# Gated mix of Hedgehog attention and a Mish MLP: a reordered third chunk of projections, and row sums kept by adding DMAs

## The chip, the core and the metric

The kernel runs on one core of a Trainium2 chip. The metric is the device time of one execution in microseconds; the median of three runs of the kernel before is 460.61 us (460.45 to 461.32).

## What is computed

`x` has 2048 rows of 512; H is 32 heads of 16 columns, F is 1376.

```
qkv   = x @ wqkv
phi_q = [softmax(q w_phi), softmax(-q w_phi)]        per head, 32 features
phi_k = [softmax(k w_phi), softmax(-k w_phi)]
kv    = sum over rows of phi_k^T v ;  z = sum over rows of phi_k
a     = (phi_q kv) / (phi_q z + 1e-6) @ wo
b     = mish(x @ w1 + b1) @ w2
out   = g a + (1 - g) b ,   g = sigmoid(x . gate_w)
```

All is float32. Each float32 operand is split into a high and a low float32r part, and a product of two operands is three products on TensorE: high with high, high with low, low with high.

## The kernel before

`w_phi` is first multiplied into the keys' and queries' weights ("fuse"). Then the rows go by in eight chunks of 256 (stage A), each chunk in two tiles of 128 rows (`t` = 0, 1). For each tile the keys `k`, the values `v` and the queries `q` are projected; `mx`, `mn`, `d0`, `d1`, `E`, `S`, `rS` and `ml` make phi_k of the keys: largest and smallest of a head, two differences into the tile `E`, its exponential on ScalarE, the sums `Sm`, their reciprocals and the scaling `ml`. Queries go to DRAM (`pqd`). `kv` multiplies `E` with the values' copy `v` into one PSUM tile `kvp`, for two chunks at a time. After that come four blocks of 512 rows (stage B), in which TensorE does `up` (x w1), `down` (w2), `num` and `wo` back to back.

Every operation is recorded under a short name and a chunk. The texts FIRST, SECOND, STRASSEN, THIRD, NEXT, LAST and BLOCK0 to BLOCK name the operations in the order in which they are issued, and each engine and each DMA queue keeps that order. In a text `'` means the chunk before, `+` the first block, `#` the weights.

**The chunks with 66 products.** Chunks 2, 3 and 4 (FAST) get keys and queries of both tiles from seven products instead of eight (Strassen's scheme). A step `s1` to `s7` is one of them: six TensorE instructions, which the helper `term` issues. The products use sums of x (`sraw`, four POOL adds in `sa`), split into `sh` (ScalarE, steps sh0 and sh1) and `sl` (POOL, sl0 and sl1), and sums of the weights (t1 to t4, split by h0 to h3 into `th` or `sh`, and by l0 to l3 into `tl` or `sl`). t2 and l2 are VectorE's, h2 is ScalarE's. The steps between the products are

- `bc`: ScalarE copies PSUM tile k0, which holds s1, to q0; s2 goes on adding to k0, and s6, s5 and s3 to q0
- `m7`: ScalarE copies s7 (`m` in the profile)
- `ca`: VectorE adds q0 and `m` into the PSUM tile of k1, to which s4 adds
- `kk`: the kv products of chunks 0 and 1 (in chunk 2) or 2 and 3 (in chunk 4)
- `v0`, `v1`: the values' projection, twelve instructions each; `ve0` and `ve1` copy it from PSUM
- `xh`, `xl`: the split of the next chunk's x on ScalarE and VectorE

Buffers matter in two places. Tiles `E` have four buffers. Tiles of tag "io" have four too: three constants of the start take the first three, then each values' copy `v` takes the next, so that the copy of chunk 2's first tile takes the buffer of chunk 0's first.

**The sums z.** `zd0` and `zd1` are DRAM tiles of 128 x 1024 (512 KB). Steps `z0` and `z1` add each `E` to them with a DMA that adds (`accum_op`; POOL issues these). In chunk 6 `zld` reads zd0 into the SBUF tile `zacc` (queue of SP), `za` adds zd1 to it with an adding DMA, and POOL adds the four `E` of chunks 6 and 7 with tensor instructions. `zh` (ScalarE) and `zl` (VectorE) split `zacc` into `zs`; `@z` in BLOCK0 is the product with ones on TensorE, whose copies to SBUF are `zb`.

Of the kernel before, what the change touches and what calls it, by code (L numbers as in the profile page):

```python
# [12 lines left out]
ALU = mybir.AluOpType  # L13
# [10 lines left out]
NCH = S // SC  # L24
# [10 lines left out]
FAST = range(2, 5)  # L35
# [6 lines left out]
    S0 rS0 ml0 S1 rS1 ml1 q0 qe0 st0 q1 qe1 st1  # L42
"""
SECOND = """
    h0# h1# l0# h3# l1# l3# z0' z1' k0 xh mx0 mn0 d00 d10 xl sa ldx k1 E0 L0# L1# mx1 mn1 d01 d11 v0 E1 S0 rS0 ve0 ml0 t2# h2# sh0 sl0 z0
    v1 S1 rS1 ml1 ve1 q0 qe0 st0 q1 sh1 sl1 qe1 st1 l2#
"""
STRASSEN = """
    s1 bc s7 m7 kk s2 xh xl sa z1' mx0 mn0 s6 ca d00 d10 E0 ldx v0 ve0 sh0 sl0 more S0 rS0 s4 mx1 mn1 s5 qa st1 d01 d11 E1 ml0 z0
    v1 S1 rS1 s3 ve1 qe0 st0 ml1 sh1 sl1  # L50
"""
THIRD = """
    k0 z1' xh xl mx0 mn0 d00 d10 ldx k1 H6# E0 O6# L8# mx1 mn1 d01 d11 v0 H7# E1 O7# L9# S0 rS0 ml0 ve0 v1 H8# O8# L10# z0
    S1 rS1 ml1 ve1 q0 qe0 st0 q1 z1 qe1 st1 kv' kv
"""
NEXT = """
    lq0+ k0 xh xl mx0 mn0 d00 d10 ldx zld k1 H9# E0 O9# ldw0 L11# mx1 mn1 d01 d11 H10# E1 O10# ldw1 za S0 rS0 ml0 z0 v0 ve0 H11# O11#
    S1 rS1 ml1 z1 v1 ve1 q0 mx0+ mn0+ d00+ d10+ qe0 st0 q1 qe1 st1 E0+ lq1+
"""
LAST = """  # L60
    k0 mx0 mn0 d00 d10 k1 E0 XH0 kv' mx1 mn1 d01 d11 E1 v0 S0 rS0 ml0 z0 ve0 ldo XH1 mx1+ mn1+ d01+ d11+ E1+
    S1 rS1 ml1 z1 XL0 XL1 v1 ve1 lq2+ q0 WH0 qe0 st0 q1 WH1 zh qe1 st1 zl kv S0+ rS0+ km
"""


# [29 lines left out]
def tile_gated_mix(ctx: ExitStack, tc: tile.TileContext, xT, wv, wkT, wqT, bd, w1a, w1b, b1, w2a, w2b, wo, out):  # L95
# [6 lines left out]
    pin = tc.keep_in_program_order  # L102
    SYNC = mybir.DependencyInfo(mybir.DependencyClass.Sync, mybir.DependencyReason.DATA)
    V, G_, A_, Sy = nc.vector, nc.gpsimd, nc.scalar, nc.sync

    def mm(*a, **k):
        return pin(nc.tensor.matmul(*a, **k))  # L107
# [14 lines left out]
    def psum(name, tag, bufs={"a": 3, "dn": 4, "kv": 1}):  # L122
        nm[0] += 1
        return pp.tile([P, 512], F32, name=f"{name}_{nm[0]}", tag=tag, bufs=bufs[tag])

    def act(out_, in_, fn=AF.Copy, **k):
        return pin(A_.activation(out_, in_, fn, **k))  # L127
# [88 lines left out]
    Z = {}  # L216
# [117 lines left out]
    def fast_ops(c, key, P_):  # L334

        def x(k, t):
            return [xs[c][i][k][:, :, t * P : (t + 1) * P] for i in range(2)]

        def s(i):
            return [SX[j][:, i, :, :] for j in range(2)]  # L340

        def term(name, a, w, start, stop):
            n = 0
            for ai, wi in ((0, 0), (0, 1), (1, 0)):
                for k in range(2):
                    mm(P_[name], a()[ai][:, k, :], w[wi][:, k, :], start=(start and n == 0), stop=(stop and n == 5), skip_group_check=True)
                    n += 1

        def new(*k, tag="a"):
            P_[k if len(k) > 1 else k[0]] = psum("proj", tag)  # L350

        def s1_():
            new("k", 0)
            new("m7", tag="dn")
            term(("k", 0), lambda: x(0, 0), wk0, True, False)

        def bc():
            new("q", 0, tag="dn")
            act(P_["q", 0], P_["k", 0])

        def s7():
            term("m7", lambda: s(0), t3, True, True)

        def m7():
            P_["m7s"] = k2("m7", "pq")
            act(P_["m7s"], P_["m7"])

        def ca():
            new("k", 1)
            pin(V.tensor_add(P_["k", 1], P_["q", 0], P_["m7s"]))  # L370
# [12 lines left out]
    def a_ops(c):
        key = ("A", c)
        P_ = psA[c] = {}
        for t in range(2):
            d = {}
            Es[c, t] = d

            def k_(t=t):  # L390
                P_["k", t] = proj(xs[c], t, wkh, wkl, "a")

            def v_(t=t):
                P_["v", t] = proj(xs[c], t, wvh, wvl, "dn" if c or t else "kv")
# [24 lines left out]
            at(key, f"ve{t}", ve)
            if t and c in FAST:  # L420
                at(key, "qa", qa)
            else:
                at(key, f"qe{t}", qe)
            at(key, f"st{t}", st)
            feat_ops(key, t, lambda t=t: P_["k", t][:, :], d, t == 1 and c in FAST)
            at(key, f"ml{t}", lambda d=d: scale_by(d, V))
            def zs(t=t, d=d):
                if c >= NCH - 2:
                    pin(G_.tensor_add(Z["acc"], Z["acc"], d["E"]))
                elif c:  # L430
                    pin(G_.dma_start(zd[t][:, :], d["E"], accum_op=ALU.add))
                else:
                    pin(G_.dma_start(zd[t][:, :], d["E"]))
# [24 lines left out]
        if odd + 1 in FAST:
            at(("A", odd + 1), "kk", kv)
        else:  # L460
            at(key, "kv", kv)
        if c in FAST:
            fast_ops(c, key, P_)
        if c + 1 in FAST:
            fast_operands(c + 1, key)
        if c + 1 < NCH:
            def xh():
                new_x(c + 1)
                for j in range(2):
# [315 lines left out]
    acc = {}  # L785
# [63 lines left out]

    run(FIRST, ("A", 0))  # L850
    run(SECOND, ("A", 1), ("A", 0))
    for c in FAST:
        w = {2: "H0# O0# L2# H1# O1# L3#", 3: "H2# O2# L4# H3# O3# L5#", 4: "H4# O4# L6# H5# O5# L7#"}[c]
        run(STRASSEN.replace("more", w), ("A", c), ("A", c - 1))
    for c, text in ((NCH - 3, THIRD), (NCH - 2, NEXT), (NCH - 1, LAST)):
        run(text, ("A", c), ("A", c - 1), ("B", 0))
    for b in range(NB):
        run((BLOCK0, BLOCK1, BLOCK, BLOCK)[b], ("B", b), ("B", b - 1), ("B", b + 1))
# [61 lines left out]
```

## Time and profile before

| what | value |
|---|---|
| median of the runs | 460.61 us |
| profiled execution | 462.78 us |
| its span | 460.7 us |
| TensorE (PE) busy | 445.1 us, 97% |
| VectorE (DVE) busy | 322.2 us, 70% |
| ScalarE (ACT) busy | 205.9 us, 45% |
| GpSimd (POOL) busy | 162.9 us, 35% |
| DMA | 47.40 MB, mean 103 GB/s |

Times in the profile's rows are microseconds from the start of the span. Stage A ends near 158 us. "PE" is TensorE, "SPq" the DMA queue of SP. A bracket at the end of a row gives the engine's idle time before it and what ended that. An adding DMA shows on POOL only as the time of its issue (some 0.9 us); when its data have landed is a row of its own in the chain of waits.

### The profile page before, as it was taken

The page shows a single profiled execution, that of the slowest core. Times are in us where ns is not written, and L with a number is a line of the kernel's source. Part 1 is how long each engine was busy: PE and PEld are TensorE (multiplying, and loading weights), DVE is VectorE, ACT ScalarE, POOL GpSimd, SP SyncE. Part 2 cuts the span into 40 slices and gives each one's busy share as a digit, 9 for nine tenths or more (in the row PEclk, how much of TensorE's full clock was granted, in tenths as well). Part 3 has the DMA queues.
Part 4 walks back from the last instruction along what each step waited for, and adds up shares of the span by engine and source line. Part 5 has one row for each costly group of instructions (what it writes and reads, how often), then busy time and mean ns, then how long its engine had stood idle before and what let it go on. Part 6 is the DMA issues. An engine that isn't in the chain of part 4 may idle for free.

```text
span 460.7 us, 7012 instructions
## 1 busy us (share of the span) xinstructions
PE 445.1 (97%) x2754; PEld 362.1 (79%) x2754; DVE 322.2 (70%) x422; ACT 205.9 (45%) x286; POOL 162.9 (35%) x115
## 2 busy tenths in 40 slices
PE   7999599999999899999899999999999999999996
PEld 7888388888888678878687887887887888787885
DVE  2498878989596999979996985747967718621002
ACT  3753544735436373735338253353354552334220
POOL 2299758835625437130204203023212121321211
PEclk9999799999999999999999999999999999999999
DMA  7310766879595210222534042323041312030002
GB/s 284 152 46 0 280 134 172 181 194 285 150 311 138 79 47 1 69 70 59 149 89 161 1 110 73 94 73 108 11 127 48 108 30 91 1 75 19 0 0 91
DMA packets 27608, 47.40 MB, mean 103 GB/s; under 512 B 5940, under 2 KB 14132, under 8 KB 27576
## 3 DMA queue, kind: packets, MB, share of 16 engines
q1 hardware_dynamic: 25528, 39.88, 28.4%
q0 software_dynamic: 1904, 6.82, 7.3%
q8 instruction: 21, 0.34, 0.3%
q10 hardware_dynamic: 144, 0.26, 0.2%
q14 instruction: 11, 0.09, 0.1%
HBM read 23.87 MB, written 14.69 MB: 84 GB/s over the span
## 4 chain that ended last, share of the span: by engine, by line
PE 71%; DVE 8%; POOL 8%; DMA 7%; issue 3%; ACT 2%; POOLq 0%
PE up L107 25%; PE down L107 24%; PE wo L107 10%; PE proj L107 9%; DMA zacc<-zd 3%; DMA zd<-E 2%; PE fuse L107 2%; PE num L107 2%; DVE Sm L275 2%; DMA raw<-in_w2a_dram 1%; DVE E L286 1%; DMA bds<-in_bd_dram 1%; PE kvp L107 1%; POOL tl L307 1%; DVE xbl L535 1%
## 5 line engine op out<-in xcount | busy, mean ns | idle before, releaser
L630 POOL TENSOR_TENSOR l<-act,h 128x512 fp32r<-128x512 f32 x44 | 61.8, 1405 | 223.1 <-ACT h L127 188.3
L127 ACT ACTIVATE act<-up,b1s 128x512 f32<-128x512 f32 x44 | 30.3, 689 | 91.5 <-PE up L107 91.3
L127 ACT ACTIVATE E<-E 128x1024 f32<-128x1024 f32 x32 | 33.7, 1062 | 59.2 <-DVE E L271 41.2
L286 DVE TENSOR_TENSOR E<-E,Sm 128x1024 f32<-128x1024 f32 x32 | 43.6, 1362 | 1.0
L275 DVE TENSOR_REDUCE Sm<-E 128x64 f32<-128x1024 f32 x32 | 38.7, 1210 | 7.3 <-ACT E L127 7.3
L107 PE MATMUL wo<-woh,ohl 128*128 128x512 f32 x128 | 40.9, 390 | 1.2 <-DVE ohl L739 1.2
L107 PE MATMUL down<-w2ah,h 128*128 128x512 f32 x96 | 37.5, 390 | 0.0
L107 PE MATMUL down<-w2ah,l 128*128 128x512 f32 x96 | 37.4, 389 | 0.0
L107 PE MATMUL down<-w2al,h 128*128 128x512 f32 x96 | 37.3, 389 | 0.0
L765 DVE SCALAR_TENSOR_TENSOR io<-down,og_sb,io 128x512 f32<-128x512 f32 x16 | 11.3, 750 | 31.1 <-PE down L107 31.0
L107 PE MATMUL down<-w2bh,h 128*128 128x512 f32 x80 | 31.2, 390 | 0.0
L107 PE MATMUL down<-w2bl,h 128*128 128x512 f32 x80 | 31.1, 389 | 0.0
L107 PE MATMUL down<-w2bh,l 128*128 128x512 f32 x80 | 31.1, 389 | 0.0
L107 PEld LDWEIGHTS wo<-woh,ohl 128*128 128x128 f32 x128 | 24.0, 188 | 6.6 <-DVE ohl L739 1.6
L127 ACT ACT_TABLE_LOAD x19 | 24.4, 1283 | 10.1 <-PE up L107 9.8
L739 DVE TENSOR_TENSOR ohl<-num,ohl 128x512 fp32r<-128x512 f32 x16 | 10.2, 678 | 26.4 <-ACT ohl L127 26.4
L127 ACT ACTIVATE h<-act 128x512 fp32r<-128x512 f32 x44 | 27.8, 632 | 1.4
L107 PE MATMUL up<-xbl,w1ah 128*128 128x512 f32 x96 | 25.8, 390 | 1.7 <-DVE xbl L535 1.7
L107 PE MATMUL up<-xbh,w1ah 128*128 128x512 f32 x96 | 26.3, 396 | 0.2 <-ACT zb L127 0.2
L535 DVE TENSOR_TENSOR xbl<-xraw,xbh 128x1024 fp32r<-128x1024 f32 x8 | 12.2, 1562 | 19.8 <-ACT xbh L127 19.8
L107 PE MATMUL up<-xbh,w1al 128*128 128x512 f32 x96 | 25.7, 389 | 0.0
L107 PE MATMUL wo<-wol,ohl 128*128 128x512 f32 x64 | 24.9, 389 | 0.0
(155 smaller groups left out, 1018.6 us busy)
## 6 DMA issues: line engine op xcount, KB each, us to landing
xraw<-in_xT_dram SPq DMA_DIRECT2D x16, 512.0 KB, 5.2
eT<-tt SPq DMA_DIRECT2D x128, 64.0 KB, 2.0
zd<-E POOLq DMA_DIRECT2D x12, 512.0 KB, 7.2
pqd<-qs SPq DMA_DIRECT2D x16, 256.0 KB, 4.7
pq<-pqd SPq DMA_DIRECT2D x16, 256.0 KB, 2.9
out_dram<-io SPq DMA_DIRECT2D x16, 256.0 KB, 2.1
raw<-in_w1a_dram SPq DMA_DIRECT2D x3, 512.0 KB, 4.3
raw<-in_w2a_dram SPq DMA_DIRECT2D x3, 512.0 KB, 4.6
```

Source lines behind the costliest of these rows:

```text
L107: return pin(nc.tensor.matmul(*a, **k))
L127: return pin(A_.activation(out_, in_, fn, **k))
L275: pin(V.tensor_reduce(d["S"], hv(d["E"][:, :]), axis=AX.X, op=ALU.add))
L286: pin(eng.tensor_mul(hv(d["E"][:, :]), hv(d["E"][:, :]), d["S"][:, :, None].to_broadcast([P, 2 * H, DH])))
L307: at("W", f"l{i}", lambda i=i, r=r: pin((V if i == 2 else G_).tensor_sub(hl[1][i], r, f32(hl[0][i]))))
L535: pin(V.tensor_sub(xb[b][1][:, :, sl], kt(raw[h], SC), f32(xb[b][0][:, :, sl])))
L630: pin(G_.tensor_sub(U[i]["l"], U[i]["a"], f32(U[i]["h"])))
L739: pin(V.tensor_sub(ohl[h, gp][:, 512:], num[h, gp], f32(ohl[h, gp][:, :512])))
L765: pin(V.scalar_tensor_tensor(io[t], dn[t], og_sb[:, i : i + 1], io[t], op0=ALU.mult, op1=ALU.add))
```

## The change

1. In chunk 1 (SECOND) x's sums `sa` are added ahead of the DMAs z0 and z1 of chunk 0; sh0 and sl0 stand ahead of t2 and h2; t2 stands behind ml1, and h2 and l2 behind st0.
2. Chunk 2 gets a text of its own (THIRD; the old THIRD is now SIXTH). It begins with s1, bc, v0, ve0; `kk` comes after `ca`; both E0 and E1 come ahead of the weights' splits H0, O0, H1 and O1.
3. `term` issues high-high, low-high, high-low instead of high-high, high-low, low-high, in all three chunks.
4. z0 and z1 of chunk 6 add to zd0 and zd1 by DMA as the earlier ones; zld and za move to chunk 7, behind ml0; z0 and z1 of chunk 7 are adding DMAs from `E` straight into `zacc`. `zh` stands behind st1, and `zl` behind the first queries' S and rS.

```
 SECOND = """
-    h0# ... l3# z0' z1' k0 xh mx0 mn0 d00 d10 xl sa ldx k1 ... S0 rS0 ve0 ml0 t2# h2# sh0 sl0 z0
-    v1 S1 rS1 ml1 ve1 q0 qe0 st0 q1 sh1 sl1 qe1 st1 l2#
+    h0# ... l3# k0 xh mx0 mn0 d00 d10 xl sa z0' z1' ldx k1 ... S0 rS0 ve0 ml0 sh0 sl0 z0
+    v1 S1 rS1 ml1 t2# ve1 q0 qe0 st0 h2# l2# q1 sh1 sl1 qe1 st1
+THIRD = """
+    s1 bc v0 ve0 s7 m7 s2 xh xl sa z1' mx0 mn0 s6 ca kk d00 d10 E0 ldx sh0 sl0 s4 mx1 mn1 s5 qa st1 d01 d11 E1 H0# O0# L2# S0 rS0 ml0 z0
+    v1 H1# O1# L3# S1 rS1 s3 ve1 qe0 st0 ml1 sh1 sl1
 STRASSEN = """
     s1 bc s7 m7 kk s2 xh xl sa z1' mx0 mn0 s6 ca d00 d10 E0 ldx v0 ve0 sh0 sl0 more S0 rS0 s4 mx1 mn1 s5 qa st1 d01 d11 E1 ml0 z0
 NEXT = """
-    lq0+ k0 ... ldx zld k1 ... ldw1 za S0 rS0 ml0 z0 v0 ve0 H11# O11#
+    lq0+ k0 ... ldx k1 ... ldw1 S0 rS0 ml0 z0 v0 ve0 H11# O11#
 LAST = """
-    k0 ... S0 rS0 ml0 z0 ve0 ldo XH1 mx1+ mn1+ d01+ d11+ E1+
-    S1 rS1 ml1 z1 XL0 XL1 v1 ve1 lq2+ q0 WH0 qe0 st0 q1 WH1 zh qe1 st1 zl kv S0+ rS0+ km
+    k0 ... S0 rS0 ml0 ldo zld za z0 ve0 XH1 mx1+ mn1+ d01+ d11+ E1+
+    S1 rS1 ml1 z1 XL0 XL1 v1 ve1 lq2+ q0 WH0 qe0 st0 q1 WH1 qe1 st1 zh kv S0+ rS0+ zl km

-            for ai, wi in ((0, 0), (0, 1), (1, 0)):
+            for ai, wi in ((0, 0), (1, 0), (0, 1)):

-                if c >= NCH - 2:
-                    pin(G_.tensor_add(Z["acc"], Z["acc"], d["E"]))
+                if c == NCH - 1:
+                    pin(G_.dma_start(Z["acc"], d["E"], accum_op=ALU.add))
                 elif c:
                     pin(G_.dma_start(zd[t][:, :], d["E"], accum_op=ALU.add))

-        if c == NCH - 2:
+        if c == NCH - 1:
             def zld():
```

On TensorE, the beginning of chunk 2 before, from s7 on (`proj_85` is s7, `kvp` the kv products of chunks 0 and 1, `proj_84` k0 with s2, `proj_86` q0 with s6, `proj_99` the first values):

```order
L107 MATMUL proj_85_530<-th_19_128,sh_21_130 128x512 x2
L107 MATMUL proj_85_530<-tl_20_129,sh_21_130 128x512 x2
L107 MATMUL proj_85_530<-th_19_128,sl_22_131 128x512 x2
L107 MATMUL kvp_88_547<-E_40_297,v_46_312 32x64 x16
L107 MATMUL kvp_88_547<-E_49_319,v_51_339 32x64 x16
L107 MATMUL kvp_88_547<-E_65_413,v_76_467 32x64 x16
L107 MATMUL kvp_88_547<-E_73_447,v_79_492 32x64 x16
L107 MATMUL proj_84_529<-wkh_11_118,xh_60_404 128x512 x2
```

The same place now, from the last of v0 (`proj_87`) to s4 (`proj_97`):

```order
L111 MATMUL proj_87_539<-wvh_13_120,xl_62_404 128x512 x2
L111 MATMUL proj_85_530<-th_19_128,sh_21_130 128x512 x2
L111 MATMUL proj_85_530<-th_19_128,sl_22_131 128x512 x2
L111 MATMUL proj_85_530<-tl_20_129,sh_21_130 128x512 x2
L111 MATMUL proj_84_529<-wkh_11_118,xh_60_402 128x512 x2
L111 MATMUL proj_84_529<-wkh_11_118,xl_62_404 128x512 x2
L111 MATMUL proj_84_529<-wkl_12_119,xh_60_402 128x512 x2
L111 MATMUL proj_86_537<-th_19_128,sh_21_130 128x512 x2
L111 MATMUL proj_86_537<-th_19_128,sl_22_131 128x512 x2
L111 MATMUL proj_86_537<-tl_20_129,sh_21_130 128x512 x2
L111 MATMUL kvp_98_594<-E_40_297,v_46_312 32x64 x16
```

v0 has moved from between s6 and s4 to ahead of s7, and kvp from behind s7 to between s6 and s4.

On ScalarE at the same time, before (`th` is h2, `proj_537<-proj_529` is `bc`, `m` is `m7`):

```order
L127 ACTIVATE th_128<-wqr_127 128x1024
L127 ACTIVATE sh_130<-sraw_418 128x512
L127 ACTIVATE v_492<-proj_475 128x512
L127 ACTIVATE qs_507<-proj_494 128x512
L127 ACTIVATE sh_130<-sraw_418 128x512
L127 ACTIVATE qs_525<-proj_510 128x512
L127 ACTIVATE proj_537<-proj_529 128x512
L127 ACTIVATE m_87_545<-proj_530 128x512
```

and now (`v_552` is the values' copy of chunk 2's first tile):

```order
L131 ACTIVATE sh_130<-sraw_416 128x512
L131 ACTIVATE v_491<-proj_473 128x512
L131 ACTIVATE qs_506<-proj_493 128x512
L131 ACTIVATE th_128<-wqr_127 128x1024
L131 ACTIVATE sh_130<-sraw_416 128x512
L131 ACTIVATE qs_526<-proj_511 128x512
L131 ACTIVATE proj_537<-proj_529 128x512
L131 ACTIVATE v_552<-proj_539 128x512
L131 ACTIVATE m_89_560<-proj_530 128x512
```

`sh` and two copies stand ahead of `th`, and the values' copy ahead of `m`.

On POOL, the sums at the end of stage A before (numbers tell the buffers apart: E_1300 and E_1333 are chunk 6, E_1446 and E_1502 chunk 7):

```order
L442 DMA zacc_1305<-zd_125 128x1024
L429 TENSOR_TENSOR zacc_1305<-zacc_1305,E_1300 128x1024
L502 TENSOR_TENSOR w2bl_1321<-raw_1327,w2bh_1320 128x512
L429 TENSOR_TENSOR zacc_1305<-zacc_1305,E_1333 128x1024
L429 TENSOR_TENSOR zacc_1305<-zacc_1305,E_1446 128x1024
L429 TENSOR_TENSOR zacc_1305<-zacc_1305,E_1502 128x1024
```

and now (E_1300 and E_1331 are chunk 6, E_1443 and E_1499 chunk 7):

```order
L435 DMA zd_124<-E_1300 128x1024
L506 TENSOR_TENSOR w2bl_1319<-raw_1325,w2bh_1318 128x512
L435 DMA zd_125<-E_1331 128x1024
L446 DMA zacc_1525<-zd_125 128x1024
L433 DMA zacc_1525<-E_1443 128x1024
L433 DMA zacc_1525<-E_1499 128x1024
```

The four adds are gone, zd takes two more DMAs, and three adding DMAs into the one tile `zacc` follow each other; zld has moved on SP's queue from ahead of the second x load of the blocks to behind the second load of wo.

More of the change, by code (lines that the diff above doesn't have):

```diff
@@ L44 @@
 SECOND = """
-    h0# h1# l0# h3# l1# l3# z0' z1' k0 xh mx0 mn0 d00 d10 xl sa ldx k1 E0 L0# L1# mx1 mn1 d01 d11 v0 E1 S0 rS0 ve0 ml0 t2# h2# sh0 sl0 z0
-    v1 S1 rS1 ml1 ve1 q0 qe0 st0 q1 sh1 sl1 qe1 st1 l2#
+    h0# h1# l0# h3# l1# l3# k0 xh mx0 mn0 d00 d10 xl sa z0' z1' ldx k1 E0 L0# L1# mx1 mn1 d01 d11 v0 E1 S0 rS0 ve0 ml0 sh0 sl0 z0
+    v1 S1 rS1 ml1 t2# ve1 q0 qe0 st0 h2# l2# q1 sh1 sl1 qe1 st1
+"""
+THIRD = """
+    s1 bc v0 ve0 s7 m7 s2 xh xl sa z1' mx0 mn0 s6 ca kk d00 d10 E0 ldx sh0 sl0 s4 mx1 mn1 s5 qa st1 d01 d11 E1 H0# O0# L2# S0 rS0 ml0 z0
+    v1 H1# O1# L3# S1 rS1 s3 ve1 qe0 st0 ml1 sh1 sl1
 """
@@ L51 @@
 """
-THIRD = """
+SIXTH = """
     k0 z1' xh xl mx0 mn0 d00 d10 ldx k1 H6# E0 O6# L8# mx1 mn1 d01 d11 v0 H7# E1 O7# L9# S0 rS0 ml0 ve0 v1 H8# O8# L10# z0
@@ L56 @@
 NEXT = """
-    lq0+ k0 xh xl mx0 mn0 d00 d10 ldx zld k1 H9# E0 O9# ldw0 L11# mx1 mn1 d01 d11 H10# E1 O10# ldw1 za S0 rS0 ml0 z0 v0 ve0 H11# O11#
+    lq0+ k0 xh xl mx0 mn0 d00 d10 ldx k1 H9# E0 O9# ldw0 L11# mx1 mn1 d01 d11 H10# E1 O10# ldw1 S0 rS0 ml0 z0 v0 ve0 H11# O11#
     S1 rS1 ml1 z1 v1 ve1 q0 mx0+ mn0+ d00+ d10+ qe0 st0 q1 qe1 st1 E0+ lq1+
@@ L60 @@
 LAST = """
-    k0 mx0 mn0 d00 d10 k1 E0 XH0 kv' mx1 mn1 d01 d11 E1 v0 S0 rS0 ml0 z0 ve0 ldo XH1 mx1+ mn1+ d01+ d11+ E1+
-    S1 rS1 ml1 z1 XL0 XL1 v1 ve1 lq2+ q0 WH0 qe0 st0 q1 WH1 zh qe1 st1 zl kv S0+ rS0+ km
+    k0 mx0 mn0 d00 d10 k1 E0 XH0 kv' mx1 mn1 d01 d11 E1 v0 S0 rS0 ml0 ldo zld za z0 ve0 XH1 mx1+ mn1+ d01+ d11+ E1+
+    S1 rS1 ml1 z1 XL0 XL1 v1 ve1 lq2+ q0 WH0 qe0 st0 q1 WH1 qe1 st1 zh kv S0+ rS0+ zl km
 """
@@ L851, in tile_gated_mix @@
     run(SECOND, ("A", 1), ("A", 0))
-    for c in FAST:
-        w = {2: "H0# O0# L2# H1# O1# L3#", 3: "H2# O2# L4# H3# O3# L5#", 4: "H4# O4# L6# H5# O5# L7#"}[c]
+    run(THIRD, ("A", 2), ("A", 1))
+    for c in FAST[1:]:
+        w = {3: "H2# O2# L4# H3# O3# L5#", 4: "H4# O4# L6# H5# O5# L7#"}[c]
         run(STRASSEN.replace("more", w), ("A", c), ("A", c - 1))
-    for c, text in ((NCH - 3, THIRD), (NCH - 2, NEXT), (NCH - 1, LAST)):
+    for c, text in ((NCH - 3, SIXTH), (NCH - 2, NEXT), (NCH - 1, LAST)):
         run(text, ("A", c), ("A", c - 1), ("B", 0))
```

## Prediction

> **What bounds the kernel now.** I read the page first, then TensorE's clock by stretches, then the timelines and the chain of waits where TensorE stands still.
>
> ```profile
> span 460.7 us, 7012 instructions
> PE 445.1 (97%) x2754; PEld 362.1 (79%) x2754; DVE 322.2 (70%) x422; ACT 205.9 (45%) x286; POOL 162.9 (35%) x115
> ```
>
> The profiled execution took 462.78 us, 2.08 more than its span; the median of the runs is 460.61. I work out shifts inside the span and add them to the median. TensorE is busy 97%, so only places where it waits can give anything, and any new wait there is paid in full. The timeline of TensorE has two such places, chunk 2 and the entry to the blocks:
>
> ```profile
> 52.89 1.22 PE L107 MATMUL proj<-th,sh 128*128 128x512 f32 x2 [4.65 <-ACT sh L127]
> ...
> 64.92 0.61 PE L107 MATMUL proj<-sh,xh 128*128 128x512 f32 x2
> ...
> 157.78 0.65 PE L107 MATMUL kvp<-E,v 128*32 128x64 f32 x32 [0.89 <-ACT qs L127]
> 162.15 1.19 PE L107 MATMUL up<-xbl,w1ah 128*128 128x512 f32 x4 [1.67 <-DVE xbl L535]
> 167.21 1.20 PE L107 MATMUL up<-xbh,w1ah 128*128 128x512 f32 x4 [0.23 <-ACT zb L127]
> ```
>
> s1 ends at 52.89 - 4.65 = 48.24 and s7 waits for `sh`; 64.92 is the start of s4. In the second place the waits are 0.89, 1.67 and 0.23. By stretches (length, busy, granted clock):
>
> ```profile
> 48.10:52.90 4.80, 0.15 (x2) 0.87 0.51 187
> 52.90:55.00 2.10, 2.06 (x4) 0.50 1.03 404
> 56.50:59.40 2.90, 2.90 (x130) 0.65 1.05 191
> ```
>
> The clock falls to half inside the long idle time: a mean of 0.87 over 4.80 us is 1.25 us at half, so it fell some 3.5 us after the idle began. It came back 0.87 us before 59.40 (0.65 over 2.90), after 5.6 us of work at half speed: a price of 2.8 us. The waits of the second place are too short for that.
>
> **Part 1: chunk 2 (THIRD, and SECOND ahead of it).** The timelines of POOL, ScalarE and VectorE (start, length, and in brackets the idle time before it and its releaser):
>
> ```profile
> 45.13 1.13 POOL L433 DMA_DIRECT2D zd<-E  x2
> 46.28 1.44 POOL L324 TENSOR_TENSOR sraw<-xraw 128x256 f32<-128x256 f32 x2
> 47.67 2.41 POOL L324 TENSOR_TENSOR sraw<-xraw,sraw 128x256 f32<-128x256 f32 x2
> 66.52 1.29 POOL L332 TENSOR_TENSOR sl<-sraw,sh 128x512 fp32r<-128x512 f32 x1 [3.55 <-PE proj L107]
> 51.26 1.06 ACT L127 ACTIVATE th<-wqr 128x1024 fp32r<-128x1024 f32 x1 [4.36 <-DVE wqr L304]
> 54.69 0.60 ACT L127 ACTIVATE proj<-proj 128x512 f32<-128x512 f32 x1
> 56.63 0.60 ACT L127 ACTIVATE m<-proj 128x512 f32<-128x512 f32 x1 [1.34 <-issue]
> 49.42 1.74 DVE L304 SCALAR_TENSOR_TENSOR wqr<-wkr,wqr 128x1024 f32<-128x1024 f32 x1
> 52.91 1.23 DVE L286 TENSOR_TENSOR E<-E,Sm 128x1024 f32<-128x1024 f32 x1
> 57.78 1.29 DVE L254 TENSOR_TENSOR xl<-xraw,xh 128x512 fp32r<-128x512 f32 x2 [1.42 <-ACT xh L127]
> 61.03 0.69 DVE L262 TENSOR_REDUCE mx<-proj 128x32 f32<-128x512 f32 x1 [1.96 <-PE proj L107]
> 62.40 0.70 DVE L370 TENSOR_TENSOR proj<-proj,m 128x512 f32<-128x512 f32 x1
> ```
>
> And from the chain of waits (start, length):
>
> ```profile
> 89.56 1.92 PE kvp L107 x128
> 172.95 2.72 PE up L107 x12
> ```
>
> Twelve products take 2.72 (0.227 each), all four quarters of kvp 1.92.
>
> - The old stall goes. POOL begins x's sums at 45.13 instead of 46.28, ends them at about 48.9, issues the two zd (1.13) and splits `sl` (1.29) by 51.35. ScalarE's `sh` no longer stands behind `th`. TensorE does v0 from 48.24 to 50.96 and then s7, to 52.3, almost without a wait.
> - What is late next is `bc`, ScalarE's copy that s2 needs, because on ScalarE it still stands behind `th`, and `th` waits for t2, which VectorE now does after S1, rS1 and ml1. Without the 1.67 of t2 ahead, ml1 (52.91 + 1.23) ends at about 52.5, or 0.4 sooner if ml0 meets less of POOL; t2's 1.74 then ends at 53.8. From `th` (51.26) to `bc` (54.69) stood six instructions in 3.43; three of the copies (0.49 each) are now ahead of `th`, so `bc` starts 1.94 after 53.9 and ends at 56.4. TensorE is idle from 52.3 to 56.4: 4.1 us, where the old stall was 4.65. Ends: 55.2 if VectorE and POOL never meet, 57.8 if each of them meets.
> - s2 and s6 (1.36 each) end at 59.2, the kvp products at 61.1. Now s4 needs `ca`, and the chain to it begins late: the values' copy ve0 stands ahead of `m` on ScalarE, and it overwrites the buffer of chunk 0's first values (four of tag "io"), which the first quarter of the delayed kvp must have read: 59.2 + 0.48 = 59.7. Then ve0 0.55, from `m` to xl 57.78 - 56.63 = 1.15, xl 1.29, from `mx` to `ca` 62.40 - 61.03 = 1.37, `ca` 0.70, and 0.1 for the hand-overs: s4 at 64.9. Queued behind ve0 are `m`, `xh` and E; v0, which filled this gap until now, has been spent.
> - At s4 the same products are done in both kernels (s1, s7, s2, s6, v0, kvp). So the place gives 64.9 - 64.92 = 0.0, between -1.2 (`bc` at 55.2) and +1.4 (57.8).
> - Clock: an idle time of 4.1 lies between waits of 1.67 that cost nothing and the one of 4.65 that cost 2.8. Both answers are open; I take the half, +1.4, and keep 0 and 2.8 (5.6 if the 3.8 us before s4 pay too).
>
> [...]
>
> Each product group in the new order needs its `xl` or `sl` 0.45 sooner and its low weights 0.45 later; from chunk 3 on `sl` (66.52) is done well ahead of its product. H0 to O1 and L2, L3 move behind E1 in chunk 2, and SP's pqd ahead of the loads; those weights are read only by the blocks. I cost all of it at nothing; if that cover is gone, a product waits for some tenths.
>
> **Part 2: the sums of the keys' features.** Removed are four POOL adds. Added are four adding DMAs, and the read-back moves from chunk 6 to chunk 7:
>
> ```profile
> 143.85 2.40 POOL L429 TENSOR_TENSOR zacc<-zacc,E 128x1024 f32<-128x1024 f32 x1 [6.63 <-DMA zacc<-zd]
> 132.12 1.28 DVE L286 TENSOR_TENSOR E<-E,Sm 128x1024 f32<-128x1024 f32 x1
> 144.24 0.32 SPq L676 DMA_DIRECT2D pq<-pqd  x1
> 147.52 2.50 SPq L550 DMA_DIRECT2D raw<-in_wo_dram  x4
> 161.05 1.06 ACT L127 ACTIVATE zs<-zacc 128x1024 fp32r<-128x1024 f32 x1 [2.35 <-POOL zacc L429]
> 162.61 1.28 ACT L127 ACT_TABLE_LOAD   x1
> 165.28 0.59 ACT L127 ACTIVATE gr<-up 1x512 f32<-1x512 f32 x1
> 166.56 1.09 ACT L127 ACTIVATE zb<-z 128x512 f32<-128x512 f32 x2 [0.69 <-PE z L107]
> ```
>
> The chain of waits, and the landing times of zd's DMAs (least, median, most), all twelve and the two plain writes of chunk 0 alone:
>
> ```profile
> 121.10 8.24 DMA zd<-E
> 129.35 6.44 DMA zacc<-zd
> 136.32 7.39 DMA zacc<-zd
> 146.28 0.69 DVE E L269
> 152.05 2.01 DVE E L269
> 162.15 3.92 PE up L107 x16
> DMA to landing us min/median/max: 3.0/7.2/10.9
> DMA to landing us min/median/max: 3.0/3.4/3.8
> ```
>
> Of the twelve, ten add. Each adding DMA waits until the one before it into the same tile has landed, so they form a chain:
>
> - z0 of chunk 6 leaves when its E is scaled, 132.12 + 1.28 = 133.4, and lands 8.24 later, at 141.6; z1 of chunk 6 follows behind the last split of w2b on POOL, some 4 to 8 us later. Both hold an E buffer that VectorE writes next (at 146.28 and 152.05); behind these waits stand ml0 and ml1 of chunk 7. By these numbers both have landed in time, and cost nothing; each us later would be paid only past 150.9, where the chain has its next member.
> - zld stands on SP behind the wo loads. Earliest 141.7; with SP as now, 144.24 + 0.32 + 2.50 = 147.1 and more. SP is freed of the old read-back at 129.35, so I take 144.4.
> - zld 6.44, to 150.9. za 7.39, to 158.3. z0 and z1 of chunk 7 add from SBUF to SBUF, which no row shows: at best the plain write's 3.4, at worst 10.9; I take 7.2, the twelve's median. They land at 165.5 and 172.7.
> - Then ScalarE does zs (1.06), and behind it in its queue the table load, up0's Mish, `h` and `gr` (162.61 to 165.87, 3.26) and zb (0.61); the third `up` needs zb's PSUM buffer. It starts at 172.7 + 1.06 + 3.26 + 0.61 = 177.6, now 167.21: +10.4. The waits of 0.89 and 1.67 that POOL's adds share in are in the old 167.21 and need no term; VectorE's xbl, now slowed beside such an add, is early, and nobody waits for that.
> - The second `up` ends at 162.15 + 3.92 = 166.07 now and, without the waits of 0.89 and 1.67, at 163.5. From there TensorE has nothing until zs ends at 173.8: 10 us, more than twice the idle time that cost it the clock: +2.8.
>
> Sum: 0.0 + 1.4 + 10.4 + 2.8 = +14.6, and 460.61 + 14.6 = 475.2. The blocks behind are bound by TensorE and give nothing back.
>
> **The rivals.**
>
> *Adds into SBUF as quick as plain writes* (3.4 each). For it: DRAM takes no part. Against: the adding read-back into SBUF took 7.39. Landing at 165.1, the third `up` at 170.0, +2.8, with half the clock's price 1.4 and part 1's 1.4: 466.2.
>
> *Faster: the whole chain hides.* From 144.4 four DMAs would have to land by 167.21 - 4.93 = 162.3, 4.5 us each; from there on the old waits (0.89 + 1.67 + 0.23 = 2.8) go as well, and with part 1 between 0 and 1.4 it takes about 458.5. Against: the two read-backs alone take 13.8 of those 17.9, and no adding row is that quick. [...]
>
> *Worse: late start and clock.* zld at 147.3 (+2.9), both idle times of chunk 2 pay (5.6 instead of 1.4): 482.3.
>
> *Part 1 gains*: ve0's buffer is free, so `ca` is done when kvp ends at 61.1, and s4 starts 3.8 sooner: 471.4. Against: four buffers, and the fifth values' tile in the row.
>
> **How the numbers follow.** Forecast 0.70, quick adds 0.10, hidden 0.04, late start 0.10, part 1 gains 0.06. The forecast is 475.2; its own range is 469 to 481 (two adds at 5.5 to 9, chunk 2 from -1.2 to +4.2). The range of 468 to 482 leaves out the quick adds, the hidden chain and half of the late start, and some of the forecast's tails: about two in ten. 0.2% (0.9 us) is about what a measurement here can tell: faster 0.04, same 0.02, slower 0.94.
>
> **What would show it.** Right: no wait at s7, one of some 4 us at s2 ended by ScalarE and one of 3 to 4 at s4; a chain zld, za, z0, z1 whose last part ends near 172, and zs near 173. Wrong: z1 of chunk 7 lands before 163, or s4 starts before 63.5.

## The result, and the profile after

The kernel after takes 478.09 us (median of four runs, 476.86 to 479.47), the kernel before beside it 460.97: a ratio of 1.0371 [1.0335, 1.0406]. The profiled execution of after took 476.86, the lowest of its four; its span is 475.1. First the page:

```profile
span 475.1 us, 7017 instructions
PE 449.9 (95%) x2754; PEld 364.2 (77%) x2754; DVE 319.7 (67%) x422; ACT 206.0 (43%) x286; POOL 154.9 (33%) x115
```

The same 2754 products take longer (449.9 busy instead of 445.1, mostly time at half clock), and the rest of the 14.4 us of span is TensorE standing still. The timeline of TensorE in chunks 2 to 4: s7, s2, kvp, s4, s1 of chunk 3, s4 of chunk 3, s1 of chunk 4, kvp of chunks 4 and 5:

```profile
50.00 0.61 PE L111 MATMUL proj<-th,sh 128*128 128x512 f32 x2
55.47 1.22 PE L111 MATMUL proj<-wkh,xh 128*128 128x512 f32 x2 [3.67 <-ACT proj L131]
60.73 1.99 PE L111 MATMUL kvp<-E,v 128*32 128x64 f32 x128
66.24 0.74 PE L111 MATMUL proj<-sh,xh 128*128 128x512 f32 x2 [3.51 <-DVE proj L374]
74.81 0.62 PE L111 MATMUL proj<-wkh,xh 128*128 128x512 f32 x2
85.47 0.74 PE L111 MATMUL proj<-sh,xh 128*128 128x512 f32 x2 [1.88 <-DVE proj L374]
92.81 0.62 PE L111 MATMUL proj<-wkh,xh 128*128 128x512 f32 x2
126.45 1.99 PE L111 MATMUL kvp<-E,v 128*32 128x64 f32 x128
```

and the rows of before at the last three boundaries:

```profile
71.72 0.61 PE L107 MATMUL proj<-wkh,xh 128*128 128x512 f32 x2
86.68 0.61 PE L107 MATMUL proj<-wkh,xh 128*128 128x512 f32 x2
120.20 1.99 PE L107 MATMUL kvp<-E,v 128*32 128x64 f32 x128
```

In after, s1 of chunk 2 starts at 45.92, before at 46.71: the start of the program was 0.8 quicker in this execution, so 0.8 is added to the times of after when the two are set side by side. Then s4 of chunk 2 is 2.1 later than before, s1 of chunk 3 is 3.9 later, s1 of chunk 4 is 6.9 later and kvp of chunks 4 and 5 is 7.0 later. What ScalarE and VectorE did ahead of the two long waits (timelines; `proj<-proj` on ScalarE is `bc`, `proj<-proj,m` on VectorE is `ca`):

```profile
52.87 1.06 ACT L131 ACTIVATE th<-wqr 128x1024 fp32r<-128x1024 f32 x1 [4.75 <-DVE wqr L308]
54.83 0.59 ACT L131 ACTIVATE proj<-proj 128x512 f32<-128x512 f32 x1
61.45 0.60 ACT L131 ACTIVATE v<-proj 128x512 f32<-128x512 f32 x1 [6.04 <-PE kvp L111]
63.09 1.29 DVE L258 TENSOR_TENSOR xl<-xraw,xh 128x512 fp32r<-128x512 f32 x2 [7.90 <-ACT xh L131]
65.50 0.69 DVE L374 TENSOR_TENSOR proj<-proj,m 128x512 f32<-128x512 f32 x1
```

`bc` stands behind `th`, which waited 4.75 for t2; and the values' copy ve0 waited for kvp, with `m`, `xh`, `xl` and `ca` in line behind it. TensorE's clock there, by stretches (length, busy, granted clock):

```profile
51.20:56.00 4.80, 1.13 (x4) 0.76 1.00 388
60.00:62.00 2.00, 2.00 (x94) 0.87 0.35 69
66.00:68.00 2.00, 1.76 (x6) 0.83 0.01 4
68.00:71.00 3.00, 3.00 (x9) 0.54 0.83 191
```

Both idle times cost the clock. It falls at about 53.7 (0.76 over 4.80 is 2.3 at half) and is back at 60.5; it falls again at 67.3, 1.1 us after work resumed at 66.24, and is back at 70.75.

The second place: SP's issue of zld, POOL's of za, the two adding DMAs into `zacc` as the chain of waits has them, and from there to the third `up`:

```profile
151.30 0.53 SPq L443 DMA_DIRECT2D zacc<-zd  x1
158.08 0.89 POOL L446 DMA_DIRECT2D zacc<-zd  x1 [11.08 <-DMA zacc<-zd]
164.05 5.44 DMA zacc<-E
170.05 4.56 DMA zacc<-E
174.72 1.06 ACT zs L131
175.83 0.79 PE L111 MATMUL z<-zs,onr 128*128 128x512 f32 x1 [6.57 <-ACT zs L131]
180.32 4.23 PE up L111 x12
```

The four links follow one another as forecast: zld lands 6.2 after its issue, za 5.4, z0 5.4 and z1 4.6, and each adding DMA leaves some 0.6 behind the landing before it. (POOL's timeline puts z0's wait down to VectorE's xbl, which ended within 0.1 of za's landing; the kernel with the sums alone, below, names za.) By the timeline the third `up` starts at 180.12, where it was 167.21, and twelve products take 4.23 instead of 2.72.

### The profile page after: what moved, and what is told of

The parts are those of the page before. It is cut to its first block, busy times and chain, and to the rows that moved or that the text cites. A ratio compares the mean times of both kernels' runs of the same rounds, so it can differ in the third digit from the quotient of the medians.

```text
span 475.1 us, 7017 instructions
## 1 busy us (share of the span) xinstructions
PE 449.9 (95%) x2754; PEld 364.2 (77%) x2754; DVE 319.7 (67%) x422; ACT 206.0 (43%) x286; POOL 154.9 (33%) x115
## 4 chain that ended last, share of the span: by engine, by line
PE 58%; DVE 5%; DMA 2%; ACT 2%; issue 0%; POOLq 0%; ACTq 0%
PE up L111 24%; PE down L111 23%; PE wo L111 9%; DMA zacc<-E 2%; PE num L111 2%; DVE Sm L279 1%; ACT L131 1%; DVE E L290 1%; DVE xbl L539 0%; DVE T L684 0%; DVE Dn L688 0%; DVE io L769 0%; DVE Sm L287 0%; DVE tt L702 0%; PE z L111 0%
## 5 line engine op out<-in xcount | busy, mean ns | idle before, releaser
L743 DVE TENSOR_TENSOR ohl<-num,ohl 128x512 fp32r<-128x512 f32 x16 | 10.3, 682 | 26.5 <-ACT ohl L131 26.4
L258 DVE TENSOR_TENSOR xl<-xraw,xh 128x512 fp32r<-128x512 f32 x14 | 16.1, 1192 | 12.0 <-ACT xh L131 12.0
```

Of the source, the lines that this page charges most:

```text
L258: low[c] = pin(eng.tensor_sub(xs[c][1][j], kt(rawx[c], SC)[:, 2 * j : 2 * j + 2, :], f32(xs[c][0][j])))
L743: pin(V.tensor_sub(ohl[h, gp][:, 512:], num[h, gp], f32(ohl[h, gp][:, :512])))
```

## The experiments

Ratios are to the kernel before, run beside each; the median of before lay between 460.97 and 461.94 throughout.

**The two parts apart.** First the kernel after with the sums z as before (zld, za, zh and zl too stand again where they stood in NEXT and LAST):

```
-                if c == NCH - 1:
-                    pin(G_.dma_start(Z["acc"], d["E"], accum_op=ALU.add))
+                if c >= NCH - 2:
+                    pin(G_.tensor_add(Z["acc"], Z["acc"], d["E"]))
```

> The changed kernel with its part on the sums put back (texts NEXT and LAST, zld and za in chunk 6, four adds on POOL); the new chunk 2, SECOND and the order of term stay. Theory (both parts cost, and add up): the chunks part costs what the shift of TensorE's rows before the blocks shows, some 6 us, so 467 us, with both waits in chunk 2 (3.7 ended by ScalarE's copy, 3.5 ended by ca) and the 1.9 in chunk 3 still there. Rival (the chain of adding DMAs is what sets the loss, and the chunks' shift would be absorbed at the entry to the blocks): 461 to 463 us.

Measured: 469.14, 1.0162 [1.0122, 1.0201]: 2 above the 467 of the theory, and far from the rival. Then the opposite, the kernel before with the sums part alone (NEXT and LAST as in after):

```
-                if c >= NCH - 2:
-                    pin(G_.tensor_add(Z["acc"], Z["acc"], d["E"]))
+                if c == NCH - 1:
+                    pin(G_.dma_start(Z["acc"], d["E"], accum_op=ALU.add))
```

> The kernel before with only the part on the sums (NEXT, LAST, zld and za in chunk 7, adding DMAs for chunk 6 into zd and for chunk 7 into zacc). Theory (the parts add up): 478.1 - 467 = 11 at most and, by the third up's shift of 12.9 less 6.0 and the clock's 1.4, some 8 us: 469 to 472 us, third up 7 us later than before, adding DMAs from SBUF to SBUF landing in 4.5 to 5.5 us each. Rival (this part is the whole loss): 475 us or more.

Measured: 470.52, 1.0192 [1.0165, 1.0219]. 1.62% and 1.92% are 3.54% together, within the intervals of the 3.71% of both: the parts add, and by these ratios they cost 7.5 and 8.9 us. In the second kernel the chain of waits shows all four links (two of zd into `zacc`, two of `E`), 6.7, 5.3, 5.4 and 4.6:

```profile
143.21 6.68 DMA zacc<-zd
150.41 5.30 DMA zacc<-zd
156.28 5.39 DMA zacc<-E
162.23 4.55 DMA zacc<-E
```

**What holds s4: ve0.** The kernel after with ve0 behind kk:

```
-    s1 bc v0 ve0 s7 m7 s2 xh xl sa z1' mx0 mn0 s6 ca kk d00 ...
+    s1 bc v0 s7 m7 s2 xh xl sa z1' mx0 mn0 s6 ca kk ve0 d00 ...
```

> The changed kernel with one step moved: in chunk 2 the values' copy ve0 stands behind kk instead of ahead of s7, so that m7 and xh no longer stand behind its wait for kvp. Theory (that wait sets the second stall of chunk 2): the wait at s4 falls from 3.5 us to under 0.5, the clock's second fall in chunk 2 goes (1.8 us), 472 to 474 us. Rival (s4 is late because its chain m7, xh, xl, mx, mn, ca starts from s6, whoever stands ahead): s4 moves by less than 1 us, 477 to 479 us.

Measured: 473.16, 1.0252 [1.0225, 1.0279], 1.2% less than after. TensorE's timeline has s4 right behind kvp (61.35 + 1.92), without a wait and at full clock (1.00 from 62 to 72):

```profile
63.27 0.73 PE L111 MATMUL proj<-sh,xh 128*128 128x512 f32 x2
```

So the wait of 3.51 and the second fall of the clock both came from one copy that overwrites a buffer which the delayed kvp still had to read.

**What holds s2: th.** The kernel after with h2 and l2 behind bc:

```
 SECOND: -  ... q0 qe0 st0 h2# l2# q1 ...     +  ... q0 qe0 st0 q1 ...
 THIRD:  -  s1 bc v0 ve0 ...                  +  s1 bc h2# l2# v0 ve0 ...
```

> The kernel after, with h2 and l2 moved from SECOND to THIRD, right behind bc: ScalarE's bc no longer stands behind th, which waits for VectorE's t2. Theory (bc was late only because th stood ahead of it): the wait of 3.67 at s2 goes; s6 then waits for th and l2, about 1 to 1.5; with so short a wait the clock doesn't fall there (2.5). The wait of 3.5 at s4 stays, since ve0 still follows the delayed kvp. About 473 to 475. Rival (t2 itself is what is late, and whoever reads th pays): the wait only moves on to s6 in full, with the clock's fall, 477 to 479.

Measured: 474.47, 1.0277 [1.0242, 1.0312]. The timeline of TensorE, s6 and s4:

```profile
54.18 0.73 PE L111 MATMUL proj<-th,sh 128*128 128x512 f32 x2 [0.75 <-ACT th L131]
61.61 1.22 PE L111 MATMUL proj<-sh,xh 128*128 128x512 f32 x2 [3.51 <-DVE proj L374]
```

The wait of 3.67 has gone; 0.75 of it moved to s6, where `th` is needed. The rival fell. The wait at s4 stayed 3.51, as expected.

**What holds chunk 3: the moved weight splits.** In after, `xl` of chunk 3 took 4.58 on VectorE, where its two halves took 1.29 in chunk 2. Beside it ran the weight split that the change had moved, and then `sl` (timelines of VectorE and POOL):

```profile
79.03 4.58 DVE L258 TENSOR_TENSOR xl<-xraw,xh 128x512 fp32r<-128x512 f32 x2
78.56 2.79 POOL L506 TENSOR_TENSOR w1al<-raw,w1ah 128x1024 fp32r<-128x1024 f32 x1
81.32 1.74 POOL L336 TENSOR_TENSOR sl<-sraw,sh 128x512 fp32r<-128x512 f32 x1
```

The experiment puts the splits back ahead of s4:

```
-    ... ldx sh0 sl0 s4 mx1 mn1 s5 qa st1 d01 d11 E1 H0# O0# L2# S0 rS0 ml0 z0
-    v1 H1# O1# L3# S1 ...
+    ... ldx sh0 sl0 H0# O0# L2# H1# O1# L3# s4 mx1 mn1 s5 qa st1 d01 d11 E1 S0 rS0 ml0 z0
+    v1 S1 ...
```

> The changed kernel with the weights' splits of chunk 2 (H0 O0 L2 H1 O1 L3) put where STRASSEN has them, ahead of s4. Theory (POOL's moved split O1 runs beside VectorE's xl of chunk 3, which took 4.58 us instead of 1.29, and so ca and s4 of chunk 3 are 1.9 us late): that wait goes, xl takes 1.3 us, 475 to 476.5 us. Rival (xl is slow for another reason, or H0 and H1 ahead of E1 make chunk 2 later by as much): 477.5 to 479 us.

Measured: 475.85, 1.0326 [1.0266, 1.0387]; against after that is not told apart from nothing. VectorE's rows for a scaling of `E` in chunk 2 and for the same `xl`:

```profile
75.05 3.24 DVE L290 TENSOR_TENSOR E<-E,Sm 128x1024 f32<-128x1024 f32 x1
81.79 1.28 DVE L258 TENSOR_TENSOR xl<-xraw,xh 128x512 fp32r<-128x512 f32 x2
```

Without POOL beside it `xl` takes 1.28: the cause of the 4.58 is shown. But it starts 2.76 later. 1.64 of that is the later start of the whole program (s1 of chunk 2 at 47.56 for 45.92); and the splits, put back, now run beside the scaling of `E` ahead of it (POOL has them from 72.43 to 77.20), which takes 3.24 where it took 1.22. So the wait at s4 of chunk 3 only falls from 1.88 to 1.32: in both places the splits met VectorE. And part of the gain in this trace lies in the clock, which didn't fall at s4 of chunk 2 behind a wait of 3.52, as long as after's (see the last section): from s4 to s1 of chunk 3 it is 6.96 where after has 8.57, some 1.6. That the splits kept it up is not shown.

**The chain's links.** The kernel after with POOL adds for the last two:

```
-                    pin(G_.dma_start(Z["acc"], d["E"], accum_op=ALU.add))
+                    pin(G_.tensor_add(Z["acc"], Z["acc"], d["E"]))
```

> The kernel after, with z0 and z1 of chunk 7 as POOL adds into zacc (2.40 each in the trace of before) in place of the two adding DMAs from SBUF (5.44 and 4.56 in the chain of after); zld and za stay in chunk 7. Theory (the second place is the length of the chain, link by link): za lands at 164.0 as now, the adds end near 169, zs starts some 5.5 sooner (174.7 now), TensorE's idle time ahead of the z product falls from 6.57 to about 1, the clock stays up (1.5): 470 to 472. Rival (the late start of the chain alone sets it, or VectorE beside POOL takes the gain back): 475 to 478.

Measured: 470.84, 1.0187 [1.0155, 1.0219]. POOL's two adds and TensorE's wait for zs:

```profile
164.72 4.86 POOL L433 TENSOR_TENSOR zacc<-zacc,E 128x1024 f32<-128x1024 f32 x2 [4.52 <-DMA zacc<-zd]
170.72 0.51 PE L111 MATMUL z<-zs,onr 128*128 128x512 f32 x1 [0.71 <-ACT zs L131]
```

4.86 takes the place of the 10.6 that the two DMAs held (164.05 to 170.05 + 4.56), the wait of 6.57 falls to 0.71, and the first z product runs at full clock. Counted from kvp's start, the third `up` begins 6.0 sooner, 5.7 of them the links': the place is worth what its links sum to. The clock did not stay up as the theory had it: with waits of 0.76 and 1.51 around the z products it falls near 174 (the first four `up` take 1.91, where before's took 1.20), and the twelve `up` products take 4.00.

**The clock's price, in the second place.** The kernel after with products that nobody reads ahead of the z products:

```
+            idle = psum("idle", "dn")
             for a in range(2):
+                for _ in range((27, 5)[a]):
+                    mm(idle, onr, xb[0][0][:, 0, :], start=True, stop=True)
```

> The kernel after, with 27 and 5 products of ones with x that nobody reads ahead of the two pairs of z products, to keep TensorE at work through its 6.57 us of idle time; the waits for zs stay. Theory (the idle time costs a second time through the clock: the twelve up products behind it took 4.23 at half clock where 2.72 is their time): the granted clock stays near 1 from 170 to 184 and the time falls by 1.5 to 2, to 476.0 to 476.8. Rival (the clock's fall is hidden, since ScalarE's chain from zs to zb sets the third up, or the products themselves are in the way): no change within 0.5, or slower by up to 1.

Measured: 475.29, 1.0291 [1.0254, 1.0327]. The 27 added products take 6.28, and TensorE waits 0.40 for zs instead of 6.57. The third `up` in the chain of waits:

```profile
179.94 2.90 PE up L111 x12
```

Its twelve products took 2.90 where after's took 4.23, and counted from kvp's start it also begins 0.4 sooner: the trace shows some 1.8, as expected. The median is below the expected 476.0 to 476.8: the ratio fell by 0.8%, with an uncertainty of half a per cent, which holds the 0.4% that 1.8 is.

**The clock's price, in the old stall.** The same in the kernel before, ahead of s7 of chunk 2:

```
         def s7():
+            for _ in range(18 if c == 2 else 0):
+                mm(P_["m7"], x(0, 0)[0][:, 0, :], wk0[0][:, 0, :], start=True, stop=True)
```

> The kernel before with 18 products of x with the keys' weights ahead of s7 of chunk 2, into the PSUM tile that s7 then overwrites; nobody reads them. They take about 4.1 of the 4.65 in which TensorE waits for sh. Theory (the idle time costs a second time through the clock, 2.8 in the trace of before): sh still ends the wait at the same time, the clock stays at 1 through s7 and kvp, 457.8 to 458.8. Rival (what follows s7 is bound by ScalarE and VectorE, so that faster products only wait longer): 460 to 461.5.

Measured: 460.07, 0.9986 [0.9968, 1.0003]. The clock stays at 1 (a mean of 1.0), but s7's last term now waits 1.23 for `sl` where it had waited 0.37:

```profile
54.56 0.73 PE L107 MATMUL proj<-th,sl 128*128 128x512 f32 x2 [1.23 <-POOL sl L332]
55.22 1.99 PE L107 MATMUL kvp<-E,v 128*32 128x64 f32 x128
```

s4 comes 1.45 sooner (62.72, with 0.75 for the earlier start, for 64.92), not 2.8: 0.86 of the rest is the longer wait for `sl`. The theory held in part, and the time is the rival's; 1.45 is 0.3%, which the interval holds.

**Three moves towards a better version.** The kernel after with the old sums z, t2 ahead of chunk 1's `xl`, h2 and l2 early there, and ve0 behind kk (the removed places are those of the change):

```
+    ... xh mx0 mn0 d00 d10 t2# xl sa z0' z1' ldx k1 E0 h2# L0# L1# mx1 mn1 d01 d11 l2# v0 ...
+    s1 bc v0 s7 m7 s2 xh xl sa z1' mx0 mn0 s6 ca kk ve0 d00 ...
```

> The kernel after with the sums part as before and three moves in the texts: t2 ahead of xl in chunk 1, with h2 behind E0 and l2 behind d11 there, so that th is ready early and bc stands behind nothing; and ve0 of chunk 2 behind kk. Theory (those two places are all that the new order of chunk 2 lost): both waits of chunk 2 and both falls of the clock go (3.67 + 3.52 + 2.5 + 1.8 from the 469.1 of the chunks alone), 457 to 460, faster than before by 1 to 4. Rival (VectorE, with t2 ahead of chunk 1's xl, becomes late there, so the wait moves into chunk 1 or on to chunk 3): 461 to 465.

Measured: 461.83, 1.0009 [0.9983, 1.0035]: the rival. The timeline of TensorE has new waits for VectorE, ahead of s2:

```profile
48.16 0.69 PE L111 MATMUL proj<-wkh,xh 128*128 128x512 f32 x2 [1.95 <-DVE E L275]
```

At s4 of chunks 2 and 3 stand 1.50 and 1.86, ended by `ca`, and in the kvp products of chunk 4 stands 2.38, ended by a scaling of `E`. VectorE is busy 75.15 of the 80 us from 25 to 105 here (69.10 in before): the old wait of chunk 2 and both falls of the clock are gone, and waits for VectorE have taken their place.

**x's sums sooner, and nothing else.** The kernel before, with its order of kvp and v0 and its sums z; the second edit holds for chunk 2 alone:

```
-    ... l3# z0' z1' k0 ... xl sa ldx ... ml0 t2# h2# sh0 sl0 z0
-    v1 S1 rS1 ml1 ve1 q0 ... qe1 st1 l2#
+    ... l3# k0 ... xl sa z0' z1' ldx ... ml0 sh0 sl0 z0
+    v1 S1 rS1 ml1 t2# ve1 q0 ... qe1 st1
-    s1 bc s7 m7 kk s2 ...
+    s1 bc s7 m7 h2# l2# kk s2 ...
```

> The kernel before with one piece of the change alone: in SECOND sa ahead of z0 and z1 of chunk 0, sh0 and sl0 behind ml0, t2 behind ml1; and h2 and l2 stand in chunk 2 behind m7. The order of v0 and kvp, the order of the terms and the sums z are as before. Theory (the old wait of 4.65 came only from late sums; kvp behind s7 is the cover that th and l2 need, and moving it behind ca was the mistake): s7 begins about 0.8 after s1, its last term waits about 1 for sl, bc stands behind nothing, s6 and s4 wait under 0.5; 5 to 6 with the clock's 2.8 are gained in chunk 2 and a part is given back in chunks 3 and 4, where VectorE comes late: 456 to 459. Rival (VectorE, 94% busy from 25 to 95 us in the kernel with three moves, gives it all back): 460.5 to 462.

Measured: 458.83, 0.9939 [0.9918, 0.9959]: 0.6% faster than before, small but outside the noise. TensorE's timeline, s7's last term and kvp:

```profile
50.84 1.22 PE L107 MATMUL proj<-th,sl 128*128 128x512 f32 x2 [2.19 <-POOL sl L332]
51.99 3.06 PE L107 MATMUL kvp<-E,v 128*32 128x64 f32 x128
```

s7 starts at once; one wait of 2.19 is left of 4.65, and chunks 2 to 7 show no other until the blocks. The 2.19 still cost the clock (0.50 from 51.5 to 54): 3.06 for kvp instead of 1.92. That may be why it stayed at the far end of what was expected.

**Taking that wait away.** On POOL the two DMA issues (1.13) stand ahead of `sl`. Here they follow it:

```
-  ... xl sa z0' z1' ldx ... ml0 sh0 sl0 z0 / ... sh1 sl1 qe1 ...
+  ... xl sa ldx ... ml0 sh0 sl0 z0' z1' / ... sh1 sl1 z0 qe1 ...
```

> As the kernel with the sums alone sooner (458.83), but on POOL the two DMAs z0 and z1 of chunk 0 stand behind sl0 instead of ahead of it, and z0 of chunk 1 behind sl1. Theory (the wait of 2.19 for sl is POOL's issue of these DMAs, 1.13, ahead of sl's 1.27, and the kvp products of 3.06 behind it run at half clock because of that wait): the wait falls to about 1.1, too short for the clock to fall, kvp takes 1.9: 1.1 + 1.1 + 0.4 less, 456.0 to 457.5. Rival (z0 and z1 now land later and hold the tiles E that chunk 2 writes, or VectorE gives it back): 458.5 to 460.

Measured: 461.88, 1.0007 [0.9987, 1.0027], more than either expectation. In chunk 2 the theory held (a wait of 1.06, kvp 2.00 at full clock). But z0 of chunk 0 now landed at 59.24; VectorE's write of `E` waited 0.66 for it, and POOL's next adding DMA left only at 59.78. So POOL came to its two weight splits 0.85 later than in the kernel with the sums alone sooner (65.47 for 64.62), and VectorE, which a clock that stayed up brings on sooner, came to its scaling of `E` 0.5 sooner (66.45 for 66.94), now behind both splits. The rows are s4 of chunk 3, the scaling and the second split:

```profile
78.26 1.08 PE L107 MATMUL proj<-sh,xh 128*128 128x512 f32 x2 [2.87 <-DVE proj L370]
66.45 5.16 DVE L286 TENSOR_TENSOR E<-E,Sm 128x1024 f32<-128x1024 f32 x1
67.84 2.68 POOL L502 TENSOR_TENSOR w1al<-raw,w1ah 128x1024 fp32r<-128x1024 f32 x1
```

The last two in the kernel with the sums alone sooner, where VectorE came first by 0.04 and POOL's second split took 3.44:

```profile
66.94 1.22 DVE L286 TENSOR_TENSOR E<-E,Sm 128x1024 f32<-128x1024 f32 x1
66.98 3.44 POOL L502 TENSOR_TENSOR w1al<-raw,w1ah 128x1024 fp32r<-128x1024 f32 x1
```

Last, only z1 of chunk 0 behind `sl`, against the version with the sums sooner:

```
-    ... xl sa z0' z1' ldx ... ml0 sh0 sl0 z0
+    ... xl sa z0' ldx ... ml0 sh0 sl0 z1' z0
```

> As the kernel with the sums alone sooner (458.83), but only z1 of chunk 0 stands behind sl0 on POOL; z0 of chunk 0, whose tile E chunk 2 writes first, stays ahead of it. Theory (a DMA issue of 0.56 less ahead of sl shortens s7's wait from 2.19 to about 1.6, too short for the clock to fall, and no tile E is late): 456.5 to 458. Rival (a shift of half a us brings VectorE's scalings beside POOL's weight splits, as in the kernel with sl first, where one took 5.16 instead of 1.22): 459 to 462.

Measured: 459.52, 0.9949 [0.9928, 0.9971]: the rival's range, and not told apart from the version with the sums sooner. The wait fell to 1.63 and the clock stayed up (1.99 for kvp), but kvp of chunk 4 waits for VectorE:

```profile
89.08 0.65 PE L107 MATMUL kvp<-E,v 128*32 128x64 f32 x32 [2.42 <-DVE E L286]
```

The best versions are this one and the one with x's sums sooner alone, both with the old order of kvp and v0, 0.5% and 0.6% under the kernel before.

## Why the prediction was right

The time was right; two groups of its terms were not, and it was luck that their errors cancelled: part 1 with its clock was forecast at 1.4 and took 7.0, part 2 with its clock at 13.2 and took 8.2. Forecast 14.6. The trace: 7.0 for part 1, 6.7 for the chain and 1.5 for the clock behind it are 15.2, less the 0.8 of the earlier start 14.4, the difference of the spans. The medians differ by 17.1, above all because the profiled execution of after is 1.2 below its median and that of before, 462.78, is 1.8 above the 460.97; why the executions differ is in no trace.

- *The old stall goes, `bc` is late next.* Right: no wait at s7, and 3.67 at s2, ended by ScalarE (forecast 4.1). Shown by moving h2.
- *ve0 and the buffer hold s4.* Right: 3.51 (forecast 3.8), shown by moving ve0. s4 came 2.1 later; without the clock's 2.5 of the next point it is 0.4 sooner, forecast 0.0.
- *Clock in chunk 2, "I take the half, +1.4".* Mis-sized. Both idle times paid: s2 and s6 took 5.26 (55.47 to 60.73) for 2.72, 2.5 up to s4, and 1.8 behind it (66.24 to 74.81 are 8.57, where 64.92 to 71.72 were 6.80), 4.3 in all; the case in brackets, 5.6, was the nearer. The clock fell 1.9 into the first idle time (51.8 to 53.7), where in before it fell some 3.5 into it, and 1.1 behind the end of the second. The second fall isn't a matter of the wait's length alone: with the splits put back, a wait of 3.52 at the same s4 kept the clock.
- *Moved splits and term order, "I cost all of it at nothing"; "some tenths" if the cover is gone.* Failed. Chunk 3 took 18.00 (74.81 to 92.81) where it took 14.96 (71.72 to 86.68): 3.0, of which the waits for `bc` and for VectorE are 0.16 and 1.88. The remaining 1.0 lies in shorter gaps, which were not followed up. `xl` beside the moved split is shown, and so is that putting the split back only moves the collision; of the order of the terms nothing was tried by itself.
- *Sums of chunk 6 by DMA cost nothing; zld at 144.4.* Right. zld left at 151.30, less 6.25 that kvp is later, 145.05.
- *za 7.39, z0 and z1 7.2 each.* Mis-sized. From issue to the next step za took 5.97 (158.08 to 164.05), z0 6.00 and z1 4.67 (to zs at 174.72): 16.6 for 21.8. zld took 6.78 for 6.44. The lower bound, a plain write's 3.4, wasn't met either. From zs to the third `up` it took 5.40 for 4.93, since the z products ran at half clock. Together +6.7 for +10.4.
- *Clock in the second place, +2.8.* Mis-sized: it fell, but cost 1.5 (4.23 for 2.72): of the 10.3 at half clock (173.1 to 183.4) TensorE was busy for 5.9, 2.6 of them with z products, between which it waited 0.52 and 1.17 for VectorE and ScalarE. In the old stall too the products that kept the clock up gave 1.45, not 2.8.
- *The old waits go.* Right: 0.89, 1.67 and 0.23 are gone.

Of the rivals, quick adds and a hidden chain fell with the 4.6 to 5.4 of the adding DMAs; an early s4 fell with the 3.51. Of the late start the clock came true (both idle times of chunk 2 paid), the late zld did not.

## What to carry to other kernels

A step moved off a wait takes its own dependences along: before moving it, look up what it was hiding (kvp hid `th` and the values' copy) and which buffer it frees. Where an engine is busy nine tenths of a stretch (VectorE here, 75.15 of 80 us), expect a gap closed on another engine to open again further on (here as 1.50, 1.86 and 2.38); and a sum of parts that comes out right should still be checked term by term, since here errors of 5 us each way met.

## What was not expected of the hardware

- The length of a wait alone doesn't tell whether the clock falls. Waits of 2.38 (three moves) and 2.42 (z1 behind `sl`) kept it, with pairs of products at 0.62 soon behind them; one of 2.19 (x's sums sooner) lost it. At s4 of chunk 2 a wait of 3.51 lost it in after, and one of 3.52 kept it with the splits put back. At s4 of chunk 3 a wait of 1.88 kept it in after (1.00 from 78.45 to 92.81), and one of 1.86 lost it with ve0 later, 0.8 after work had resumed. Once down, it stayed at half for 6.8, 3.4 and 10.3 in after (53.7 to 60.5, 67.3 to 70.75, 173.1 to 183.4). What decides is not shown. The rows are s4 and the fourth pair from it, in chunk 2 with the splits put back (kept, 0.62) and in chunk 3 with ve0 later (lost, 1.05):

```profile
68.33 0.74 PE L111 MATMUL proj<-sh,xh 128*128 128x512 f32 x2 [3.52 <-DVE proj L374]
69.83 0.62 PE L111 MATMUL proj<-th,sh 128*128 128x512 f32 x2
80.89 0.72 PE L111 MATMUL proj<-sh,xh 128*128 128x512 f32 x2 [1.86 <-DVE proj L374]
83.00 1.05 PE L111 MATMUL proj<-th,sh 128*128 128x512 f32 x2
```

- In before, after and the kernel with the sums alone, adding DMAs of 512 KB into `zacc` took 5.3 to 7.4 from DRAM, and in the last two 4.6 to 5.4 from SBUF: leaving DRAM out saved little. The plain read zld took 6.2 to 6.7, so it isn't shown that the adding is what costs. The plain write's 3.4 isn't a fixed price either: the two plain writes of chunk 0, which the change issues at 48.10 instead of 45.13, landed after 5.8 and 10.0 in after; SP issued the loads of x and w1 at the same time (from 48.19), but that these are the cause was not tried.
- VectorE and POOL slowed each other where their instructions ran at the same time. In the kernel with `sl` first a scaling of `E` took 5.16 beside two POOL splits, where it took 1.22; POOL's split took 3.44 where VectorE's scaling had started 0.04 ahead of it, and 2.39 just before that (the kernel with the sums alone sooner). In the first case POOL's second split started at 67.84 and took 2.68, all within the scaling's 66.45 to 71.61.
